# First MoE layer of a fused attention and MoE kernel: steps of group 0 in two halves around group 1, and GpSimd's part of the weight split moved to VectorE

## The chip, the cores and the metric

The kernel runs on one core of one Trainium2 chip. The metric is the device time of one execution in microseconds (us): 1056.31 us, the median of 3 runs (1056.09 to 1056.58). Engines are named as in the profile: PE is TensorE (PEld its weight loads), DVE is VectorE, ACT is ScalarE, POOL is GpSimd, SP is SyncE, which issues the DMAs spoken of here.

## The reference, cut to what matters

Three layers follow each other over 2304 tokens (4 batches of 576) of width 512: attention with a window of 64, a dense MoE layer of 2048 hidden columns with a squared relu, and a second MoE layer of 8 experts with the two best per token.

```
attn_out = _attn_ref(**attn_kwargs)                    # q, k, v: 4 x 8 heads x 576 x 64, float32
x = attn_out.transpose(0, 2, 1, 3).reshape(B * S, H * D)   # 2304 x 512
h = np.maximum(x @ w_in, 0.0)                          # first MoE: w_in 512 x 2048
x = (h * h @ w_out).astype(np.float32)                 #            w_out 2048 x 512
return _moe2_ref(x=x, **moe2_kwargs)                   # gate, noise, top 2 of 8 experts, w1, w2
```

w_in and w_out are float32 draws times a NumPy scalar of type float64, so they arrive in float64: 8 bytes a number.

## The kernel before, in words

Every matrix product is made of three products of rounded parts: an operand x is split into a rounded high part and the rest (x minus the high part), and high x high, high x rest and rest x high are added in PSUM.

**First MoE.** The tokens are cut into 6 groups of 384 (g = 0 to 5), the hidden columns into 16 blocks of 128 (f = 0 to 15). A step (g, f) has two halves. `L1(g, f)` multiplies block f of w_in with the group's tokens (12 matmuls of 384 columns into a PSUM tile "h"), then takes the relu on ACT into r, the square on ACT into the high part h[:, 0], the square again in full precision into r, and the rest h[:, 1] on DVE. `L2(g, f)` multiplies h with block f of w_out and adds to three PSUM tiles "o" (9 matmuls of 512 columns). PE's order is L1(g, f), filler, L2 of the step before, filler. After f = 15 the three sums of a group are copied to SBUF tiles "x2" and written to a DRAM tensor `x2d`, from which the second MoE gathers its rows.

**Weights.** All 32 blocks (16 of w_in, 16 of w_out; the text calls each a half) are loaded once, by `moe1_load` on SP's queue, 512 KB each, and stay in SBUF. A half is converted from float64 to float32 in `f64_to_f32` by one ACT operation (L159) and three DVE operations on integers (L160, L161, L162) into a tile "x2" or "cv", and then split by `split`: ACT writes the high part (L148), POOL the rest (L149). `weights(n)` converts halves until n are there; it is called in group 0 at the head of L1(0, f) with n = 2f + 6, so two halves are converted per step up to f = 13.

**Filler.** Between the halves of a step stand pieces of other work, taken in turn from generators: `att_group(g + 1)`, the attention of the next group (8 units of 4 pieces, each with PE, ACT, DVE and one POOL multiplication, L268), and `gating(g - 1)` of the group before. `filler(-(-left[0] // slots))` spreads what is left over the remaining slots of the group.

**What sets the order.** The Python code gives a program order; the framework then orders each engine's instructions by its own schedule. Each engine runs its queue in order and waits on semaphores.

**Second MoE.** From about 530 us: one pass after another over the experts, with POOL doing the rest of the weight split and the gathers.

Of the kernel before, what the change touches and what calls it, by code (L numbers as in the profile page):

```python
# [8 lines left out]
F32 = mybir.dt.float32  # L9
F32R = mybir.dt.float32r  # L10
# [6 lines left out]
REST = 4  # L17
# [14 lines left out]
AHEAD = 6  # L32
# [8 lines left out]
def moe_kernel(ctx, tc, q, k, v, w_in, w_out, wg, wn, noise, w1, w2, out):  # L41
    nc = tc.nc
    B, H, S, D = q.shape
    N, DM = out.shape
    E, _, F2 = w1.shape
    F = w_out.shape[0]
    NCC = DM // 128
# [96 lines left out]
                              pn[:, :N // 128 * E].rearrange("p (e t) -> p e t", e=E))  # L144


    def split(dst, src):
        nc.scalar.activation(dst[:, 0], src, AF.Copy)  # L148
        nc.gpsimd.tensor_sub(dst[:, 1], src, dst[:, 0].bitcast(F32))  # L149

    wide = w_in.dtype != F32
    if wide:
# [2 lines left out]
    def f64_to_f32(w):  # L155
        hi, lo = w[:, :, 1], w[:, :, 0]
        i = len(wres) % (3 + CVB)
        a = hw.tile([128, 512], I32, name="x2", bufs=3) if i < 3 else stg.tile([128, 512], I32, name="cv", bufs=CVB)
        nc.scalar.activation(a.bitcast(F32), hi.bitcast(F32), AF.Abs, scale=2.0 ** -112)  # L159
        nc.vector.tensor_scalar(a, a, 3, 0x7FFFFFFF, op0=OP.logical_shift_left, op1=OP.bitwise_and)  # L160
        nc.vector.scalar_tensor_tensor(a, hi, -0x80000000, a, op0=OP.bitwise_and, op1=OP.bitwise_or)  # L161
        nc.vector.scalar_tensor_tensor(a, lo, 29, a, op0=OP.logical_shift_right, op1=OP.bitwise_or)  # L162
        return a.bitcast(F32)
# [14 lines left out]
    def moe1_half(f, second):  # L178
        if 2 * f + second not in loaded:
            moe1_load(2 * f + second)  # L180
        st = loaded.pop(2 * f + second)
        w = (ringa if f < NF2 else ringb).tile([128, 2, 512], F32R, name="w")
        split(w, f64_to_f32(st.rearrange("p (a b) -> p a b", b=2)) if wide else st)
        return w

    wres = {}
# [3 lines left out]
    def weights(n):  # L190
        for x in worder[len(wres):n]:
            wres[divmod(x, 2)] = moe1_half(*divmod(x, 2))
# [100 lines left out]
    def att_group(g):  # L293
        xTs[g] = xtp.tile([128, 2, NCC, TG], F32R, name="xT")
        pool, bank = (att, ps) if g else (att0, lambda _: ps(next(late_tags if begun else start_tags)))
        lags = LAG if g else LAG0
        units = []

        def load_v(u):
            for load in late.pop(u, ()):  # L300
                load()

        for step in range(UG + max(lags)):
            for lag in lags:
                i = step - lag
                if not 0 <= i < UG:
                    continue
                if lag == 0:
                    u = g * UG + (i if g else ORD[i])
                    for x in range(u, min(u + 2, NU)) if g else ():  # L310
                        if x not in lds:
                            b, r = divmod(x, NSB * HP)
                            lds[x] = att_loads(b, r // HP, 2 * (r % HP), 2, pool)
                    if i < 2:
                        load_v(u)
                    qbd = qbds[u % 2] if g else qbds[2 + i % 4]
                    units.append(att_unit(u, lds.pop(u), xTs[g], pool, qbd, bank))
                next(units[i])
                if lag == max(lags) and g and i + 2 < UG:
                    load_v(g * UG + i + 2)  # L320
                yield
# [18 lines left out]
    def accumulate(o, steps, first, last):  # L340
        terms = [(i, t, hi, wi) for i in range(len(steps)) for hi, wis in ((0, (0, 1)), (1, (0,)))
                 for t in range(len(o)) for wi in wis]
        for i, t, hi, wi in sorted(terms, key=lambda x: (x[1], x[0])) if last else terms:
            h, w = steps[i]
            hs = h[:, hi, 128 * t:min(128 * t + 128, h.shape[2])]
            nc.tensor.matmul(o[t][:hs.shape[1]], hs, w[:, wi], start=(first and i == 0 and hi == 0 and wi == 0),  # L346
                             stop=(last and i == len(steps) - 1 and hi == 1))

    def L1(g, f):
        if g == 0:  # L350
            weights(2 * f + AHEAD)
        ph, c = begun.pop(f) if f in begun else (ps("h"), 0)
        products(ph, TG, wres[f, 0], xTs[g], range(c, NCC))
        r = hw.tile([128, TG], F32, name="r", bufs=1)
        h = hw.tile([128, 2, TG], F32R, name="h")
        nc.scalar.activation(r, ph[:, :TG], AF.Relu)  # L356
        nc.scalar.activation(h[:, 0], r, AF.Square)  # L357
        (nc.vector if g else nc.gpsimd).tensor_mul(r, r, r)  # L358
        nc.vector.tensor_sub(h[:, 1], r, h[:, 0].bitcast(F32))  # L359
        L1out[g, f] = h  # L360

    def L2(g, f):
        if f == 0:
            outs[g] = [ps("o") for _ in range(TT)]
        o = outs[g]
        accumulate(o, [(L1out.pop((g, f)), wres[f, 1])], f == 0, f == NF - 1)
        if f == NF - 1:
            x2s[g] = []
            for t in range(TT):
                x2 = hw.tile([128, DM], F32, name="x2", bufs=3)  # L370
                if t == 1:
                    nc.scalar.activation(x2, o[t], AF.Copy)
                else:
                    nc.vector.tensor_copy(x2, o[t])
                nc.sync.dma_start(x2d[TG * g + 128 * t:TG * g + 128 * t + 128, :], x2)
                x2s[g].append(x2)


# [151 lines left out]
    def stage2(e, f):  # L530
        pool = M2["stg"]
        st = pool.tile([128, 1024], F32, name="st2")
        nc.sync.dma_start(st[:, :512].rearrange("p (c f) -> p c f", c=NCC),
                          w1[e, :, 128 * f:128 * f + 128].rearrange("(c p) f -> p c f", p=128))
        nc.sync.dma_start(st[:, 512:], w2[e, 128 * f:128 * f + 128, :])
        ws = []
        for i in range(2):
            w = ringa.tile([128, 2, 512], F32R, name="w")
            split(w, st[:, 512 * i:512 * i + 512])
            ws.append(w)  # L540
        return ws

# [86 lines left out]
    def add_fill(gen, n):  # L629
        fill.append(gen)  # L630
        left[0] += n

    def filler(n):
        while n > 0 and fill:
            gen = fill.pop(0)
            try:
                next(gen)
                n -= 1
                left[0] -= 1
                fill.append(gen)  # L640
            except StopIteration:
                pass

    def drain():
        filler(10 ** 6)
        left[0] = 0

    def clear_out():
        zero = hw.tile([128, DM], F32, name="x2", bufs=3)
        nc.vector.memset(zero, 0.0)  # L650
        rows = lambda x: x.rearrange("(t p) d -> p t d", p=128)
        nc.sync.dma_start(rows(out), zero[:, None, :].to_broadcast([128, N // 128, DM]))
        nc.sync.dma_start(rows(x2d[N - TG:, :]), zero[:, None, :].to_broadcast([128, TT, DM]))
# [25 lines left out]
    att0.release()  # L679
    ringb = tc.alloc_tile_pool(name="ringb", bufs=2 * (NF - NF2), reuse_waits="tile")  # L680
    prev = None
    for g in range(NG):
        drain()
        if g == 1:
            stg.release()
            GAT["pool"] = tc.alloc_tile_pool(name="gat", bufs=1)
        if g == NG - 1:
            att.release()
            gxp = tc.alloc_tile_pool(name="gxp", bufs=1, side="right")
            gx = []  # L690
            for j in range(CT):
                t = gxp.tile([128, DM], F32, name=f"gx{j}")
                nc.vector.memset(t, 0.0)
                gx.append(t)
            M2["stg"] = tc.alloc_tile_pool(name="stg2", bufs=2, side="right")
        if g + 1 < NG:
            add_fill(att_group(g + 1), 4 * UG)
        for f in range(NF):
            if g == NG - 1 and f >= 2 and f - 2 < NF2:
                w2s[0, f - 2] = stage2(0, f - 2)  # L700
            if g == 0 and f == NF - 3:
                late_consts()
            if g == 1 and f == 8:
                clear_out()
            slots = 2 * (NF - f)
            L1(g, f)
            filler(-(-left[0] // slots))
            if prev:
                L2(*prev)
            if f == 0 and g > 0:  # L710
                add_fill(gating(g - 1), 6 + 2 * REST)
            if f == NF - 1 and g == NG - 1:
                drain()
                index_tables(0, TT)
                xA = xtp.tile([128, 2, NCC, TG], F32R, name="xT")
                add_fill(prep(list(range(TT)), xA), TT)
            filler(-(-left[0] // (slots - 1)))
            prev = (g, f)
    drain()
    L2(*prev)  # L720

# [167 lines left out]
```

## Time and profile before

| what | value |
|---|---|
| median of 3 runs | 1056.31 us |
| the profiled execution's own time | 1056.97 us |
| its span in the trace | 1055.0 us |
| PE busy over the span | 1017.3 us, 96% |
| DVE, ACT, POOL busy | 509.1, 417.8, 409.6 us |
| mean granted TensorE clock | 0.991 of full speed |

The trace covers 1055.0 us of the 1056.97 us; the other 2 us lie around it. Busy time of PE counts overlapping pipelined matmuls as one stretch. A share over the whole span is a mean over stages with different limits, so the table does not say where time can be had; stretches do.

### The profile page before, as it was taken

How to read it: one execution, taken by the hardware profiler on the slowest of the kernel's cores; microseconds unless marked ns; L12 is line 12 of the kernel's file. 1: busy time of each engine (PE TensorE's matmuls, PEld its weight loads, DVE VectorE, ACT ScalarE, POOL GpSimd, SP SyncE). 2: the span in 40 equal slices, each digit the busy share in tenths (PEclk: the TensorE clock that was granted, in tenths of full speed). 3: DMA queues.
4: the chain of work that ended last, by engine and by line, in shares of the span. 5: the costliest groups of instructions: out<-in, count | busy, mean ns of one | idle time of the engine just before them, and what ended most of it. 6: DMA issues, size and time to landing. Idle time of an engine off the chain costs nothing.

```text
span 1055.0 us, 16793 instructions
## 1 busy us (share of the span) xinstructions
PE 1017.3 (96%) x6120; PEld 899.5 (85%) x6120; DVE 509.1 (48%) x1195; ACT 417.8 (40%) x1037; POOL 409.6 (39%) x405
## 2 busy tenths in 40 slices
PE   8877799999999999999989999999999999999997
PEld 6656688889888988888878889998898998998996
DVE  7999977436645744753773642131312222231312
ACT  4664555335434443533532335332333233333210
POOL 3565631100200210110260059766565756565411
PEclk9998999999999999999999999999999999999999
DMA  9655546212112111211330326444343444443111
GB/s 200 178 160 159 164 105 235 47 30 70 39 33 78 31 39 48 54 32 23 111 111 1 110 92 194 154 140 150 117 156 106 153 134 132 128 134 121 46 47 47
DMA packets 148736, 108.33 MB, mean 103 GB/s; under 512 B 85753, under 2 KB 126713, under 8 KB 148651
## 3 DMA queue, kind: packets, MB, share of 16 engines
q1 hardware_dynamic: 139451, 80.09, 26.8%
q0 software_dynamic: 9200, 27.14, 8.2%
q8 instruction: 50, 0.82, 0.3%
q14 instruction: 35, 0.29, 0.1%
HBM read 89.27 MB, written 20.48 MB: 104 GB/s over the span
## 4 chain that ended last, share of the span: by engine, by line
PE 78%; DVE 10%; issue 6%; ACT 2%; POOL 1%; DMA 1%; POOLq 0%; SPq 0%; ACTq 0%; DVEq 0%
PE h L329 34%; PE o L346 27%; PE att L346 6%; PE att L255 2%; PE att L283 2%; DVE x L161 2%; PE att L564 2%; DVE x L162 1%; PE att L272 1%; DVE h L359 1%; DVE x L160 1%; PE att L396 1%; ACT P L265 1%; DVE r L358 1%; POOL out_dram L552 1%
## 5 line engine op out<-in xcount | busy, mean ns | idle before, releaser
L346 PE MATMUL o<-w,h 128*128 128x512 f32 x1488 | 391.4, 401 | 16.8 <-DVE h L359 12.4
L346 PEld LDWEIGHTS o<-w,h 128*128 128x128 f32 x1488 | 269.8, 189 | 74.4 <-DVE h L359 16.2
L329 PE MATMUL h<-xT,w 128*128 128x384 f32 (+1 forms) x1344 | 262.8, 343 | 3.2 <-DVE xT L287 1.9
L329 PEld LDWEIGHTS h<-xT,w 128*128 128x128 f32 x1344 | 230.4, 191 | 8.6 <-POOL w L149 2.5
L149 POOL TENSOR_TENSOR w<-st,w 128x512 fp32r<-128x512 f32 x128 | 165.1, 1301 | 104.6 <-ACT w L148 66.5
L329 PE MATMUL h<-x2T,w 128*128 128x312 f32 x1344 | 201.4, 306 | 0.0
L329 PEld LDWEIGHTS h<-x2T,w 128*128 128x128 f32 x1344 | 195.8, 188 | 3.6
L583 DVE SCALAR_TENSOR_TENSOR h<-h 128x312 fp32r<-128x312 f32 (+2 forms) x128 | 61.9, 483 | 272.7 <-ACT h L582 272.7
L148 ACT ACTIVATE w<-st 128x512 fp32r<-128x512 f32 x128 | 80.8, 631 | 191.3 <-PE att L346 119.7
L268 POOL TENSOR_TENSOR P<-P,stat 128x384 f32<-128x384 f32 x48 | 41.7, 871 | 219.4 <-DVE stat L267 103.9
L356 ACT ACTIVATE r<-h 128x384 f32<-128x384 f32 x96 | 46.7, 486 | 142.6 <-PE h L329 123.3
L582 ACT ACTIVATE h<-h 128x312 fp32r<-128x312 f32 (+2 forms) x128 | 54.4, 425 | 116.5 <-PE h L329 116.5
L346 PE MATMUL att<-w,h 128*128 128x512 f32 (+1 forms) x336 | 94.3, 393 | 0.0
L358 DVE TENSOR_TENSOR r<-r 128x384 f32<-128x384 f32 x80 | 53.0, 662 | 69.9 <-ACT h L357 68.6
L346 PEld LDWEIGHTS att<-w,h 128*128 128x128 f32 (+1 forms) x336 | 61.0, 181 | 15.4
L359 DVE TENSOR_TENSOR h<-r,h 128x384 fp32r<-128x384 f32 x96 | 60.5, 630 | 4.9 <-POOL r L358 2.2
L546 POOL DMA_INDIRECT gx<-x2d,ix x40 | 40.9, 1022 | 49.2 <-PE att L564 40.8
L552 POOL DMA_INDIRECT out_dram<-y,ix x35 | 34.4, 984 | 44.1 <-DVE y L594 37.2
L357 ACT ACTIVATE h<-r 128x384 fp32r<-128x384 f32 x96 | 50.2, 523 | 1.5
L265 ACT ACTIVATE P<-P,stat 128x128 f32<-128x128 f32 x96 | 37.6, 392 | 28.1 <-DVE stat L263 23.6
L149 POOL TENSOR_TENSOR w<-x,w 128x512 fp32r<-128x512 f32 x24 | 35.4, 1479 | 27.0 <-ACT w L148 26.8
L546 POOL DMA_INDIRECT gy<-out_dram,ix x35 | 35.6, 1016 | 19.8 <-issue 19.7
(208 smaller groups left out, 988.1 us busy)
## 6 DMA issues: line engine op xcount, KB each, us to landing
st<-in_moe_w_dram SPq DMA_DIRECT2D x128, 256.0 KB, 3.1
st<-in_moe_w_in_dram SPq DMA_DIRECT2D x16, 512.0 KB, 4.3
st<-in_moe_w_out_dram SPq DMA_DIRECT2D x16, 512.0 KB, 3.6
vn<-in_v_dram SPq DMA_DIRECT2D x110, 64.0 KB, 2.2
x2d<-x SPq DMA_DIRECT2D x18, 256.0 KB, 2.7
out_dram<-x SPq DMA_DIRECT2D x1, 4608.0 KB, 15.3
qn<-in_q_dram SPq DMA_DIRECT2D x40, 96.0 KB, 2.5
kn<-in_k_dram SPq DMA_DIRECT2D x28, 128.0 KB, 2.8
```

Source lines behind the costliest of these rows:

```text
L148: nc.scalar.activation(dst[:, 0], src, AF.Copy)
L149: nc.gpsimd.tensor_sub(dst[:, 1], src, dst[:, 0].bitcast(F32))
L265: nc.scalar.activation(P[:, j], src[:, j], AF.Exp, bias=st[:, j, 0:1], accum_out=st[:, j, 1:2])
L329: nc.tensor.matmul(p[:, :n], w[:, wi, 128 * c:128 * c + 128], x[:, xi, c], start=(c == 0 and i == 0), stop=(c == NCC - 1 and i == 2))
L346: nc.tensor.matmul(o[t][:hs.shape[1]], hs, w[:, wi], start=(first and i == 0 and hi == 0 and wi == 0), stop=(last and i == len(steps) - 1 ...
L356: nc.scalar.activation(r, ph[:, :TG], AF.Relu)
L357: nc.scalar.activation(h[:, 0], r, AF.Square)
L358: (nc.vector if g else nc.gpsimd).tensor_mul(r, r, r)
L359: nc.vector.tensor_sub(h[:, 1], r, h[:, 0].bitcast(F32))
L546: nc.gpsimd.indirect_dma_start(out=dst, out_offset=None, in_=src[:, :], in_offset=bass.IndirectOffsetOnAxis(ap=slot[i][0][:dst.shape[0]], ...
L582: nc.scalar.activation(h[:, 0, a:a + m], ph[:, :m], AF.Relu)
L583: nc.vector.scalar_tensor_tensor(h[:, 1, a:a + m], ph[:, :m], 0.0, h[:, 0, a:a + m].bitcast(F32), op0=OP.max, op1=OP.subtract)
```

## The change

Two things are changed together. First, who computes: the rest of the weight split in the first MoE (L149) goes from POOL to DVE (the second MoE's split stays on POOL), and the full-precision square becomes one DVE operation in all groups, r = h x r with h read from PSUM (it was r x r from SBUF, on POOL in group 0 and on DVE elsewhere). Second, the order: the steps run (0, 0..7), (1, 0..15), (0, 8..15), then groups 2 to 5 as before. Group 0's sums over f = 0..7 are written to `x2d`, read back at (0, 12), and added to those over f = 8..15. `weights` is called behind h, with two halves per step in (0, 0..7) and one per step from (1, 0) on. The attention of group 1 is spread over the 8 steps (0, 0..7), that of group 2 over the 8 steps (0, 8..15); group 1 has neither attention nor gating as filler. gating(1) starts at (0, 8), gating(0) at (2, 0).

```diff
-    def split(dst, src):
+    def split(dst, src, engine):
         nc.scalar.activation(dst[:, 0], src, AF.Copy)
-        nc.gpsimd.tensor_sub(dst[:, 1], src, dst[:, 0].bitcast(F32))
+        engine.tensor_sub(dst[:, 1], src, dst[:, 0].bitcast(F32))
...
     def L1(g, f):
-        if g == 0:
-            weights(2 * f + AHEAD)
...
-        (nc.vector if g else nc.gpsimd).tensor_mul(r, r, r)
+        nc.vector.tensor_mul(r, ph[:, :TG], r)
         nc.vector.tensor_sub(h[:, 1], r, h[:, 0].bitcast(F32))
         L1out[g, f] = h
+        weights(wneed.get((g, f), 0))
+
+    NH = NF // 2
+    steps = ([(0, f) for f in range(NH)] + [(1, f) for f in range(NF)] + [(0, f) for f in range(NH, NF)]
+             + [(g, f) for g in range(2, NG) for f in range(NF)])
+    wneed = {x: 2 * x[1] + AHEAD for x in steps[:NH]}
+    wneed.update({(1, f): 2 * NH + AHEAD + f for f in range(NF)})
...
+    def fetch_part():
+        for t in range(TT):
+            x2 = hw.tile([128, DM], F32, name="x2", bufs=3)
+            nc.sync.dma_start(x2, rows(0, t))
+            part.append(x2)
...
     def L2(g, f):
+        first = f == 0 or (g, f) == (0, NH)
+        last = f == NF - 1 or (g, f) == (0, NH - 1)
...
+                x2 = part[t] if part and g == 0 else hw.tile([128, DM], F32, name="x2", bufs=3)
+                if part and g == 0:
+                    nc.vector.tensor_add(x2, o[t], x2)
...
+            nxt = {(0, 0): 1, (0, NH): 2}.get((g, f), g + 1 if g > 1 else NG)
+            if nxt < NG:
+                add_fill(att_group(nxt), 4 * UG)
...
+        slots = 2 * n_left
+        L1(g, f)
+        filler(-(-left[0] // slots))
+        if prev:
+            L2(*prev)
+        if (g, f) == (0, NH + 4):
+            fetch_part()
+        done = {(0, NH): 1, (2, 0): 0}.get((g, f), g - 1 if f == 0 and g > 2 else None)
+        if done is not None:
+            add_fill(gating(done), 6 + 2 * REST)
```

The constants of the second MoE's gate (`late_consts`) move from (0, 13) to (1, 13), and the clearing of the output from (1, 8) to (2, 8). Line numbers of the changed kernel differ: L160 to L162, L148, L149, L243, L263 to L268 and L287 are the same; the square is L356 on DVE, the rest of h is L357 (L358 and L359 before).

In DVE's queue, these are the rows behind one rest of h (L359) in group 0 before the change; x and cv are the float32 tiles of a half, w its split, att and stat tiles of the attention.

```order
L359 TENSOR_TENSOR h<-r,h 128x384
L161 SCALAR_TENSOR_TENSOR cv<-st,cv 128x512
L266 TENSOR_SCALAR stat<-stat 128x3
L243 TENSOR_SCALAR qbd_106<-att 64x3x64
L162 SCALAR_TENSOR_TENSOR cv<-st,cv 128x512
L267 RECIPROCAL stat<-stat 128x3
L243 TENSOR_SCALAR qbd_106<-att 64x3x64
L160 TENSOR_SCALAR x_710<-x_710 128x512
L161 SCALAR_TENSOR_TENSOR x_710<-st,x_710 128x512
L263 TENSOR_REDUCE stat<-att 128x3
```

And this is the same queue in a step of (0, 0..7) after the change, from the rest of h (L357) to the next square (L356).

```order
L357 TENSOR_TENSOR h<-r,h 128x384
L161 SCALAR_TENSOR_TENSOR x_873<-st,x_873 128x512
L160 TENSOR_SCALAR cv<-cv 128x512
L162 SCALAR_TENSOR_TENSOR x_873<-st,x_873 128x512
L161 SCALAR_TENSOR_TENSOR cv<-st,cv 128x512
L243 TENSOR_SCALAR qbd_106<-att 64x3x64
L149 TENSOR_TENSOR w<-x_873,w 128x512
L162 SCALAR_TENSOR_TENSOR cv<-st,cv 128x512
L243 TENSOR_SCALAR qbd_106<-att 64x3x64
L263 TENSOR_REDUCE stat<-att 128x3
L149 TENSOR_TENSOR w<-cv,w 128x512
L287 TENSOR_TENSOR xT<-att,xT 128x192
```

The rest of the split (L149) now stands in DVE's queue, two instructions behind the L162 on which ACT's high part waits, and a whole attention unit stands in each step.

In PE's queue, the end of group 0 and the head of group 1 look like this before the change (L234 to L283 are attention, L387 is gating).

```order
L346 MATMUL o<-w,h 128x512 x9
L283 MATMUL att<-PT,vn 64x64 x6
L329 MATMUL h<-xT,w 128x384 x12
L234 MATMUL att<-ident,qn 128x96 x2
L236 MATMUL att<-ident,kn 128x128 x2
L346 MATMUL o<-w,h 128x512 x9
L253 LDWEIGHTS ident_b
L253 MATMUL att<-mask_89,ident_b 128x384
L255 MATMUL att<-kT,qbd_104 128x128 x3
L329 MATMUL h<-xT,w 128x384 x12
```

After the change, the head of the second half of group 0 reads as follows (L407 and L416 are gating of group 1).

```order
L346 MATMUL o<-w,h 128x512 x9
L255 MATMUL att<-kT,qbd_104 128x128 x3
L329 MATMUL h<-xT,w 128x384
L407 MATMUL att<-ident,x_1980 128x128 x4
L234 MATMUL att<-ident,qn 128x96 x2
L236 MATMUL att<-ident,kn 128x128 x2
L329 MATMUL h<-xT,w 128x384 x11
L407 MATMUL att<-ident,x_1983 128x128 x4
L255 MATMUL att<-kT,qbd_106 128x128 x3
L407 MATMUL att<-ident,x_1986 128x128 x4
```

Three pieces of filler stand there between the halves of a step where one or two stood; in group 1 between, L329 and L346 follow each other with none.

## Rows read from the trace of the kernel before

**Rows 1.** The page, part 2: busy tenths in 40 slices of 26.4 us.
```profile
PE 8877799999999999999989999999999999999997
DVE  7999977436645744753773642131312222231312
POOL 3565631100200210110260059766565756565411
```

**Rows 2.** Stretches: length, busy us of PE, PEld, DVE, ACT, POOL; clock, DMA share, GB/s.
```profile
40.00:94.60 54.60, 42.90 (x237) 34.49 (x236) 51.82 (x77) 31.69 (x84) 32.65 (x30) 0.97 0.59 172
94.60:149.00 54.40, 46.69 (x276) 38.64 (x276) 48.46 (x70) 29.52 (x74) 32.99 (x32) 0.94 0.48 132
149.00:238.00 89.00, 89.00 (x571) 78.82 (x569) 50.43 (x148) 39.37 (x114) 10.39 (x16) 1.00 0.37 110
238.00:326.80 88.80, 88.80 (x569) 78.74 (x568) 49.46 (x145) 38.86 (x113) 10.34 (x15) 1.00 0.19 47
```

**Rows 3.** Who waited for whom, 40 to 149 us: total us, times, longest.
```profile
POOL w L149 <- ACT w L148: 27.9, 15, 2.8
...
PE o L346 <- DVE h L359: 12.2, 6, 4.3
...
DVE stat L266 <- ACT P L265: 2.7, 3, 1.1
```

**Rows 4.** Groups by line and shape, 40 to 95 us: busy us, mean ns | idle before.
```profile
L149 POOL TENSOR_TENSOR w<-x,w 128x512 fp32r<-128x512 f32 x11 | 16.8, 1526 | 11.7 <-ACT w L148 11.5
L161 DVE SCALAR_TENSOR_TENSOR x<-st,x 128x512 int32<-128x512 int32 x12 | 15.1, 1258 | 0.2
...
L148 ACT ACTIVATE w<-x 128x512 fp32r<-128x512 f32 x11 | 6.9, 629 | 14.2 <-DVE x L162 14.2
...
L268 POOL TENSOR_TENSOR P<-P,stat 128x384 f32<-128x384 f32 x5 | 4.2, 833 | 5.7 <-DVE stat L267 2.9 <-ACT x L159 2.8
...
L243 DVE TENSOR_SCALAR qbd<-att 64x192 f32<-64x192 f32 x11 | 3.9, 352 | 0.2
...
L263 DVE TENSOR_REDUCE stat<-att 128x3 f32<-128x384 f32 x5 | 2.8, 561 | 0.2
```

**Rows 5.** Timeline of DVE, then of POOL, 31 to 36 us: start, us, instruction.
```profile
31.55 0.42 DVE L160 TENSOR_SCALAR x<-x 128x512 int32<-128x512 int32 x1
31.88 0.35 DVE L287 TENSOR_TENSOR xT<-att,xT 128x192 fp32r<-128x192 f32 x1
32.15 0.68 DVE L161 SCALAR_TENSOR_TENSOR x<-st,x 128x512 int32<-128x512 int32 x1
32.75 1.50 DVE L160 TENSOR_SCALAR cv<-cv 128x512 int32<-128x512 int32 x1
...
32.37 1.59 POOL L149 TENSOR_TENSOR w<-x,w 128x512 fp32r<-128x512 f32 x1 [2.16 <-ACT w L148]
```

**Rows 6.** Groups by line and shape, 590 to 800 us, then 240 to 330 us.
```profile
L583 DVE SCALAR_TENSOR_TENSOR h<-h 128x384 fp32r<-128x384 f32 x7 | 3.9, 555 | 6.1 <-ACT h L582 6.1
...
L358 DVE TENSOR_TENSOR r<-r 128x384 f32<-128x384 f32 x16 | 9.5, 596 | 11.0 <-ACT h L357 10.7
...
L391 DVE TENSOR_TENSOR x2T<-att,x2T 128x512 fp32r<-128x512 f32 x3 | 2.1, 689 | 0.2
```

**Rows 7.** Timeline of PE: L2(0,0), L2(0,7), L1(1,0), L1(2,0), a bare step's start and the next.
```profile
40.05 1.68 PE L346 MATMUL o<-w,h 128*128 128x512 f32 x6
...
94.56 0.72 PE L346 MATMUL o<-w,h 128*128 128x512 f32 x2 [0.50 <-ACT h L357]
...
149.06 0.44 PE L329 MATMUL h<-xT,w 128*128 128x384 f32 x1
...
238.01 0.51 PE L329 MATMUL h<-xT,w 128*128 128x384 f32 x2
...
560.53 2.27 PE L329 MATMUL h<-xT,w 128*128 128x384 f32 x12
...
564.72 2.27 PE L329 MATMUL h<-xT,w 128*128 128x384 f32 x12
```

More of the change, by code (lines that the diff above doesn't have):

```diff
@@ L182, in moe1_half @@
         w = (ringa if f < NF2 else ringb).tile([128, 2, 512], F32R, name="w")
-        split(w, f64_to_f32(st.rearrange("p (a b) -> p a b", b=2)) if wide else st)
+        split(w, f64_to_f32(st.rearrange("p (a b) -> p a b", b=2)) if wide else st, nc.vector)
         return w
@@ L357, in L1, with rows @@
         nc.scalar.activation(h[:, 0], r, AF.Square)
-        (nc.vector if g else nc.gpsimd).tensor_mul(r, r, r)
+        nc.vector.tensor_mul(r, ph[:, :TG], r)
         nc.vector.tensor_sub(h[:, 1], r, h[:, 0].bitcast(F32))
         L1out[g, f] = h
+        weights(wneed.get((g, f), 0))
[4 more added lines that the diff above has]
+    wneed.update({(1, f): 2 * NH + AHEAD + f for f in range(NF)})
+    part = []
+    def rows(g, t):
+        return x2d[TG * g + 128 * t:TG * g + 128 * t + 128, :]
+    def fetch_part():
[3 more added lines that the diff above has]
+            part.append(x2)
     def L2(g, f):
-        if f == 0:
+        first = f == 0 or (g, f) == (0, NH)
+        last = f == NF - 1 or (g, f) == (0, NH - 1)
+        if first:
             outs[g] = [ps("o") for _ in range(TT)]
         o = outs[g]
-        accumulate(o, [(L1out.pop((g, f)), wres[f, 1])], f == 0, f == NF - 1)
-        if f == NF - 1:
+        accumulate(o, [(L1out.pop((g, f)), wres[f, 1])], first, last)
+        if last:
             x2s[g] = []
             for t in range(TT):
-                x2 = hw.tile([128, DM], F32, name="x2", bufs=3)
-                if t == 1:
+                x2 = part[t] if part and g == 0 else hw.tile([128, DM], F32, name="x2", bufs=3)
+                if part and g == 0:
+                    nc.vector.tensor_add(x2, o[t], x2)
+                elif t == 1:
                     nc.scalar.activation(x2, o[t], AF.Copy)
@@ L374, in L2 @@
                     nc.vector.tensor_copy(x2, o[t])
-                nc.sync.dma_start(x2d[TG * g + 128 * t:TG * g + 128 * t + 128, :], x2)
+                nc.sync.dma_start(rows(g, t), x2)
                 x2s[g].append(x2)
@@ L538, in stage2 @@
             w = ringa.tile([128, 2, 512], F32R, name="w")
-            split(w, st[:, 512 * i:512 * i + 512])
+            split(w, st[:, 512 * i:512 * i + 512], nc.gpsimd)
             ws.append(w)
@@ L681, in moe_kernel @@
     prev = None
[L682 to L718, printed above, removed]
@@ new lines, in moe_kernel @@
+    left_f = {}
+    for i, (g, f) in enumerate(steps):
+        n_left = 1
+        while i + n_left < len(steps) and steps[i + n_left][0] == g:
+            n_left += 1
+        if f == 0 or (g, f) == (0, NH):
+            drain()
+            if (g, f) == (0, NH):
+                stg.release()
+                GAT["pool"] = tc.alloc_tile_pool(name="gat", bufs=1)
+            if g == NG - 1:
+                att.release()
+                gxp = tc.alloc_tile_pool(name="gxp", bufs=1, side="right")
+                gx = []
+                for j in range(CT):
+                    t = gxp.tile([128, DM], F32, name=f"gx{j}")
+                    nc.vector.memset(t, 0.0)
+                    gx.append(t)
+                M2["stg"] = tc.alloc_tile_pool(name="stg2", bufs=2, side="right")
+            nxt = {(0, 0): 1, (0, NH): 2}.get((g, f), g + 1 if g > 1 else NG)
+            if nxt < NG:
+                add_fill(att_group(nxt), 4 * UG)
+        if g == NG - 1 and f >= 2 and f - 2 < NF2:
+            w2s[0, f - 2] = stage2(0, f - 2)
+        if (g, f) == (1, NF - 3):
+            late_consts()
+        if (g, f) == (2, 8):
+            clear_out()
+        slots = 2 * n_left
[8 more added lines that the diff above has]
+            add_fill(gating(done), 6 + 2 * REST)
+        if f == NF - 1 and g == NG - 1:
+            drain()
+            index_tables(0, TT)
+            xA = xtp.tile([128, 2, NCC, TG], F32R, name="xT")
+            add_fill(prep(list(range(TT)), xA), TT)
+        filler(-(-left[0] // (slots - 1)))
+        prev = (g, f)
```

## The prediction

> **What bounds the kernel now.** The slices of the page come first: from about 130 us on PE is at 9 tenths in nearly every slice, but between 50 and 130 us it stands at 7 while DVE stands at 9 [rows 1]. So I cut the first MoE into stretches. Groups 1 and 2 take 89.0 and 88.8 us with PE busy throughout and DVE at 50 us. Group 0 does not: from L2(0,0) at 40.05 to L2(0,7) at 94.56 us DVE is busy 51.8 of 54.6 us and PE 42.9, and from there to L1(1,0) at 149.06 PE is busy 46.7 of 54.4 [rows 2, 7]. The waits tell the same: PE waited 12.2 us for DVE's last step of h [rows 3]. A bare step of PE, without filler, takes 564.72 - 560.53 = 4.19 us [rows 7], so 16 of them are 67.0 us and attention plus gating take the other 21.8 us of a full group. From L2(0,0) to L1(1,0) lie 109.0 us with 14.5 steps and one attention, 60.8 + at most 21.8 = 82.6 us of PE's work. The 26 us between are what can be had there.
>
> Why is DVE full there? Not by its own work alone. The timeline shows an integer operation of 512 columns taking 0.68 us, and the next one starting 0.60 us after it; L160 takes 0.42 us (0.33 to the next start) and L287 0.35 us (0.27). But the L160 at 32.75 us, issued while POOL runs an L149 from 32.37 to 33.96, takes 1.50 us [rows 5]. Between 40 and 95 us L161 takes 1.26 us in the mean [rows 4]. DVE operations between SBUF tiles stand still while POOL works; those that read PSUM do not (L243, from PSUM, keeps 0.35 us, L263 0.56 [rows 4]).
>
> How much? The order before gives DVE between the ends of h(0,0) and h(0,7) 14 L160, 14 L161, 14 L162, 7 L359, 11 L243, 5 each of L263, L266 and L267, and one L287. I count each by its start-to-start time, the duration less 0.08 us as in rows 5: 14 x 0.33 + 28 x 0.60 + 7 x 0.475 + 11 x 0.27 + 5 x 0.48 + 5 x 0.25 (L266 with L267, an estimate below L287's) + 0.27 = 31.6 us. Busy were 51.8, so 20.2 us were standing still against 32.65 us of POOL's work [rows 2]: 0.62 us lost on DVE per us of POOL.
>
> **The change part by part.**
>
> *Start, to L2(0,0).* Four L149 come to DVE (4 x 0.61 = 2.4 us) and four L149 with the first square leave POOL (about 6.5 us x 0.62 = 4 us). I take 0, bounds -2 to +2.
>
> *Steps (0, 0..7), DVE.* The order after has, between the same two ends of h, 12 L160, 13 L161, 13 L162, 14 L149, 7 squares from PSUM, 7 rests, 16 L243, 8 each of L263, L266 and L267, and 5 L287. L149 on DVE is not in the trace. Its nearest rows are L161 undisturbed, 0.68, and L391, also a subtraction of 512 columns, 0.689 [rows 5, 6]; I take 0.61 between starts, bounds 0.60 and 0.69. The square from PSUM times SBUF has its row in L583 at 384 columns: 0.555 us, against L358's 0.596 [rows 6], so 0.475 between starts. Sum: 4.0 + 15.6 + 8.5 + 6.65 + 4.3 + 3.8 + 2.0 + 1.35 = 46.2 us. POOL keeps 8 multiplications of 0.833 us [rows 4] and eight small memsets, about 8.7 us, which cost 8.7 x 0.62 = 5.4 us. DVE sat idle 2.8 us before; with POOL's share of the chain now its own I take 4. Total 55.6 us against 54.5: **+1.1 us**, though these 7 steps now hold all of group 1's attention where before they held some five of eight units. Below, PE bounds it: 7 x 4.19 + 21.8 = 51 us, or some 48 if the gating in the 21.8 is worth 3. Above: durations in place of starts (117 operations x 0.08 = 9), POOL's time lost whole (3), 10 us idle, together 74 us. I stay near the low side, since the value is calibrated on the same stretch. ACT (31.7 us before, three more units) and the DMA engines (0.59 of 54.6 us; about 17 us of DMA time for a whole group's attention by group 2's 0.19) stay below 45 us [rows 2].
>
> [...]
>
> *From L2(0,7) to L1(2,0).* Before: 238.01 - 94.56 = 143.45 us [rows 7]. After, PE has there what it had in group 1 (attention, one gating, 16 steps: 88.95 us) and 7.5 steps more, bare: 88.95 + 31.4 = 120.4 us. On this lies what DVE cannot keep up with. In the first 8 steps of group 1 DVE has 13 L160, 12 each of L161, L162 and L149, 16 operations of h, 2 copies of group 0's sums and 3 L287, by the same prices 35.7 us, with 2 us idle 37.7, against 33.5 of bare PE: +4.2. In the other 8 DVE has hardly a conversion left: 0. In (0, 8..15) there are three pieces of filler per slot, and the chain of gating has half the steps to hide in; DVE's work there (49.5 us of a full group less 16 operations of h, about 40) fits in 57. I take +3 for PE waits, bounds 0 and +10. Total 127.6: **-15.9 us**.
>
> *The rest at nothing.* Two more copies of sums, three adds for three copies, 0.75 MB written and read back: the copies are counted above, the transfers have over 16 steps between write and read, and the reads 4 steps before use; SP issues them among attention loads that are wanted a step later. If the x2 tiles came free late, conversions in group 1 would wait about 3 us, inside the bounds. From L1(2,0) on the work is the same, shifted; POOL against DVE at the start of the second MoE may fall otherwise by 2 us either way.
>
> *Sum.* 1.1 - 15.9 = -14.8 us on an execution of 1056.97 us (span 1055.0): 1042.2, span 1040.2. The median lies 0.66 us below that execution, so 1041.5 us.
>
> **The rivals.**
>
> *A: the wait moves into DVE, and it is slower.* POOL waited 27.9 us, 15 times, for ACT's high part before an L149: 1.86 us each [rows 3]. L149 now stands in DVE's queue, in order. If DVE waited so long in each of the 28 L149 behind h(0,0), it would lose 52 us, 4 or so hidden in group 1: about 1090 us. It decides from 14.8 / 28 = 0.53 us each; at 0.8 us, the time is 1042 + 22 = 1064. Against it: the order puts one to three operations, 0.8 us or more, between L162 and its L149, and ACT's operation takes 0.63 us [rows 4]. For it: ACT's queue is in order too, and an L148 may stand behind exponentials.
>
> *B: the first half of group 1 and the doubled filler eat it.* With (0, 0..7) at 62 us and +5 us more in the rest the time is 1042 + 6.4 + 5 = 1053 us. For it speak the upper bounds; the point at which nothing is left is a step of 10 us in (0, 0..7).
>
> *C: PE bounds all.* If DVE's standing still vanishes with POOL's work and idle stays at 2 us, (0, 0..7) takes 49 us and the later excess halves to 3.6: 1042 - 6.6 - 3.6 = 1031 us. For it: PE and DVE counts are near each other, 48 and 46.
>
> **How the numbers follow.** Forecast 0.62 (1036 to 1048), A 0.10, B 0.14, C 0.14. The range 1030 to 1055 takes in C and B and leaves out most of A and what lies beyond C, under 2 in 10. Within 0.2% (1054.2 to 1058.4) is about what a measurement of this kernel can't tell from no change; it gets B's upper end, 0.06. Slower has A, 0.10; faster the rest, 0.84.
>
> **What would show it.** In the changed trace L161 and L162 should fall to about 0.75 us in the mean, L149 on DVE stand at 0.69 and the square at 0.55 us. L2(0,7) should stand at 95 to 97 us, L1(2,0) at 222 to 225, and PE should be busy above 95% in group 1. DVE waiting over 0.5 us for each L148 means A; PE busy under 90% in (0, 8..15) means B. The sum is wrong if the 0.62 does not carry over to a stretch in which POOL is hardly busy.

## The result and the profile after

The changed kernel takes 1043.26 us, the median of 4 runs (1042.56 to 1044.06), against 1056.20 for the kernel before beside it: a ratio of 0.9878 with a 95% interval of 0.9861 to 0.9895. It is faster by 1.2%, 12.9 us; forecast were 1041.5 us and 14.8 us of gain. The profiled execution has a span of 1041.1 us.

PE's timeline of the changed kernel gives the same marks as [rows 7]: L2(0,0), L2(0,7), the fourth L1 of group 1, L1(0,8) and L1(2,0).

```profile
39.21 0.50 PE L346 MATMUL o<-w,h 128*128 128x512 f32 x1
...
89.21 0.73 PE L346 MATMUL o<-w,h 128*128 128x512 f32 x2 [1.33 <-ACT w L148]
...
109.89 2.27 PE L329 MATMUL h<-xT,w 128*128 128x384 f32 x12
...
165.48 0.33 PE L329 MATMUL h<-xT,w 128*128 128x384 f32 x1
...
223.89 0.44 PE L329 MATMUL h<-xT,w 128*128 128x384 f32 x1
```

Against before: the start gives 0.84 us (40.05 to 39.21), the steps (0, 0..7) give 4.5 us (54.5 to 50.0), the stretch from L2(0,7) to L1(2,0) gives 8.8 us (143.45 to 134.7), and from there to the end it is 817.2 us against 817.0. The sum is 13.9 us, the difference of the spans.

The stretches between these marks, with the columns of [rows 2]:

```profile
39.20:89.20 50.00, 45.97 (x297) 36.83 (x296) 49.12 (x107) 36.44 (x103) 8.16 (x14) 1.00 0.70 198
89.20:109.90 20.70, 17.91 (x102) 14.63 (x103) 18.36 (x37) 11.61 (x28) 1.24 (x2) 0.92 0.70 216
109.90:165.50 55.60, 55.60 (x283) 50.18 (x282) 34.80 (x67) 23.55 (x45) 0.33 (x1) 1.00 0.20 59
165.50:223.90 58.40, 55.65 (x394) 48.48 (x392) 38.02 (x129) 31.40 (x96) 9.57 (x14) 1.00 0.32 80
```

In (0, 0..7) DVE is as full as before, 49.1 of 50.0 us, but POOL is busy only 8.2 us where it was 32.65, and PE now 46.0 of 50.0. The second stretch, from L2(0,7) to the fourth L1 of group 1, is called the hand-over from here on: PE is busy 17.9 of 20.7 us there, and its clock falls to 0.92 in the mean. The rest of group 1 is bare steps of PE without a gap, busy 55.6 of 55.6 us.

DVE's groups by shape in (0, 0..7), which answer to [rows 4] and [rows 6]:

```profile
L162 DVE SCALAR_TENSOR_TENSOR x<-st,x 128x512 int32<-128x512 int32 x10 | 8.7, 870 | 0.0
L161 DVE SCALAR_TENSOR_TENSOR x<-st,x 128x512 int32<-128x512 int32 x10 | 8.1, 807 | 0.0
L149 DVE TENSOR_TENSOR w<-x,w 128x512 fp32r<-128x512 f32 x10 | 6.8, 680 | 0.3 <-ACT w L148 0.3
...
L356 DVE TENSOR_TENSOR r<-h,r 128x384 f32<-128x384 f32 x7 | 3.9, 550 | 0.2 <-ACT h L355 0.2
...
L160 DVE TENSOR_SCALAR x<-x 128x512 int32<-128x512 int32 x9 | 3.7, 411 | 0.0
```

On the tiles named x, L161 fell from 1.26 to 0.81 us and L160 from 0.59 to 0.41; the L149 that came to DVE takes 0.68 us where POOL's took 1.53, and waits 0.3 us in all for ACT. The square from PSUM takes 0.55 us.

About the hand-over, PE's longest waits are one for ACT's high part of a weight half, which ends as L2(0,7) starts, and three for DVE's work, 2.3 us together (waits of PE, 86 to 112 us: total, times, longest):

```profile
PE o L346 <- ACT w L148: 1.3, 1, 1.3
PE h L329 <- DVE r L356: 1.2, 1, 1.2
PE h L329 <- DVE xT L287: 1.1, 2, 0.7
```

PE's timeline shows what was left to do when L2(0,7) began, and where PE waited for xT, the attention's result:

```profile
86.83 0.44 PE L329 MATMUL h<-xT,w 128*128 128x384 f32 x1
...
89.88 0.73 PE L283 MATMUL att<-PT,vn 128*64 128x64 f32 x12
...
93.50 0.55 PE L272 MATMUL att<-ident,P 128*128 128x128 f32 x3 [0.53 <-POOL P L268]
93.98 0.73 PE L283 MATMUL att<-PT,vn 128*64 128x64 f32 x12
...
95.07 0.73 PE L283 MATMUL att<-PT,vn 128*64 128x64 f32 x12
...
96.79 2.18 PE L329 MATMUL h<-xT,w 128*128 128x384 f32 x11 [0.33 <-DVE xT L287]
99.70 1.15 PE L329 MATMUL h<-xT,w 128*128 128x384 f32 x5 [0.73 <-DVE xT L287]
102.05 3.91 PE L329 MATMUL h<-xT,w 128*128 128x384 f32 x12 [1.19 <-DVE r L356]
```

DVE's timeline shows what stands in its queue there. After the rest of h(0,7) (L357) the conversions of two halves, six operations, come ahead of the next two xT (L287); the two L149 of these halves come ahead of the last xT. ACT's part of that last xT starts at 95.84 and takes 0.33 us, but DVE's part starts only at 99.30: the L149 before it in the queue waited for ACT's high part, and that for a weight load which ended at 96.79.

```profile
92.23 0.53 DVE L357 TENSOR_TENSOR h<-r,h 128x384 fp32r<-128x384 f32 x1
92.67 1.06 DVE L160 TENSOR_SCALAR x<-x 128x512 int32<-128x512 int32 x1
93.65 0.41 DVE L160 TENSOR_SCALAR cv<-cv 128x512 int32<-128x512 int32 x1
93.99 0.68 DVE L161 SCALAR_TENSOR_TENSOR x<-st,x 128x512 int32<-128x512 int32 x1
94.59 0.68 DVE L161 SCALAR_TENSOR_TENSOR cv<-st,cv 128x512 int32<-128x512 int32 x1
95.19 0.68 DVE L162 SCALAR_TENSOR_TENSOR x<-st,x 128x512 int32<-128x512 int32 x1
95.79 0.68 DVE L162 SCALAR_TENSOR_TENSOR cv<-st,cv 128x512 int32<-128x512 int32 x1
96.40 0.61 DVE L287 TENSOR_TENSOR xT<-att,xT 128x192 fp32r<-128x192 f32 x2
98.09 0.69 DVE L149 TENSOR_TENSOR w<-x,w 128x512 fp32r<-128x512 f32 x1 [1.09 <-ACT w L148]
98.70 0.68 DVE L149 TENSOR_TENSOR w<-cv,w 128x512 fp32r<-128x512 f32 x1
99.30 0.35 DVE L287 TENSOR_TENSOR xT<-att,xT 128x192 fp32r<-128x192 f32 x1
```

In (0, 8..15) PE waits twice for the chain of gating, now under half the steps (waits of PE, 165 to 224 us):

```profile
PE att L521 <- POOL x2T L516: 1.3, 1, 1.3
PE att L477 <- DVE cm L469: 1.3, 1, 1.3
```

### The profile page after: what moved, and what is told of

It is laid out like the page before. It is cut to its first block, busy times and chain, and to the rows that moved or that the text cites. A ratio compares the mean times of both kernels' runs of the same rounds, so it can differ in the third digit from the quotient of the medians.

```text
span 1041.1 us, 16809 instructions
## 1 busy us (share of the span) xinstructions
PE 1014.9 (97%) x6120; PEld 898.5 (86%) x6120; DVE 489.1 (47%) x1246; ACT 420.5 (40%) x1037; POOL 345.2 (33%) x357
## 4 chain that ended last, share of the span: by engine, by line
PE 81%; DVE 7%; issue 5%; DMA 2%; POOL 1%; ACT 1%; SPq 0%; POOLq 0%; ACTq 0%
PE h L329 35%; PE o L346 29%; PE att L346 6%; PE att L283 2%; PE att L255 2%; PE att L584 2%; PE att L272 1%; DMA st<-in_moe_w_in_dram 1%; PE att L416 1%; PE att L407 1%; DVE w L149 1%; DVE x L162 1%; POOL out_dram L572 1%; DVE qbd L243 1%; PE att L236 1%
## 5 line engine op out<-in xcount | busy, mean ns | idle before, releaser
L346 PE MATMUL o<-w,h 128*128 128x512 f32 x1488 | 390.1, 399 | 1.3 <-ACT w L148 1.3
L346 PEld LDWEIGHTS o<-w,h 128*128 128x128 f32 x1488 | 270.1, 188 | 54.5 <-ACT w L148 1.6
L329 PE MATMUL h<-xT,w 128*128 128x384 f32 (+1 forms) x1344 | 262.6, 341 | 2.3 <-DVE r L356 1.2
L329 PEld LDWEIGHTS h<-xT,w 128*128 128x128 f32 x1344 | 231.0, 190 | 9.2 <-DVE xT L287 1.8
L329 PE MATMUL h<-x2T,w 128*128 128x312 f32 x1344 | 201.4, 306 | 0.0
L149 POOL TENSOR_TENSOR w<-st,w 128x512 fp32r<-128x512 f32 x128 | 164.7, 1297 | 104.3 <-ACT w L148 66.6
L329 PEld LDWEIGHTS h<-x2T,w 128*128 128x128 f32 x1344 | 195.8, 188 | 3.6
L148 ACT ACTIVATE w<-st 128x512 fp32r<-128x512 f32 x128 | 80.8, 631 | 190.3 <-PE att L346 120.0
L268 POOL TENSOR_TENSOR P<-P,stat 128x384 f32<-128x384 f32 x48 | 40.9, 853 | 233.2 <-DVE stat L267 126.9
L346 PE MATMUL att<-w,h 128*128 128x512 f32 (+1 forms) x336 | 94.3, 393 | 0.0
L356 DVE TENSOR_TENSOR r<-h,r 128x384 f32<-128x384 f32 x96 | 53.2, 554 | 81.8 <-ACT h L355 80.3
L346 PEld LDWEIGHTS att<-w,h 128*128 128x128 f32 (+1 forms) x336 | 61.0, 181 | 15.4
L357 DVE TENSOR_TENSOR h<-r,h 128x384 fp32r<-128x384 f32 x96 | 56.8, 591 | 3.0
L243 DVE TENSOR_SCALAR qbd<-att 64x192 f32<-64x192 f32 x86 | 30.3, 352 | 24.3 <-PE att L236 23.4
```

The costliest lines, as they stand in the source:

```text
L149: engine.tensor_sub(dst[:, 1], src, dst[:, 0].bitcast(F32))
L329: nc.tensor.matmul(p[:, :n], w[:, wi, 128 * c:128 * c + 128], x[:, xi, c], start=(c == 0 and i == 0), stop=(c == NCC - 1 and i == 2))
L356: nc.vector.tensor_mul(r, ph[:, :TG], r)
```

## Experiments

The theory behind the prediction is called R: what group 0 loses is DVE standing still while POOL works, and the gain comes from taking POOL's work away. Its rival, O: the order of steps is what counts, since it halves the rate of conversions. The median of before was 1056.20 us beside the full change and 1057.26 to 1057.51 us in these runs, on four chips, so kernels are compared by their ratios to the kernel before.

| run | order of steps | what is on DVE | us | ratio to before, interval |
|---|---|---|---|---|
| e2_order_only | new | nothing more | 1060.94 | 1.0037, 1.0024 to 1.0049 |
| e11_behind_h_only | old, conversions behind h | nothing more | 1055.84 | 0.9977, 0.9966 to 0.9988 |
| e7b_square_only | old, conversions behind h | square | 1049.60 | 0.9919, 0.9903 to 0.9936 |
| e7a_split_only | old, conversions behind h | rest of split | 1039.70 | 0.9834, 0.9818 to 0.9851 |
| e1_engines_only | old | both | 1043.63 | 0.9864, 0.9848 to 0.9881 |
| e1b_engines_behind_h | old, conversions behind h | both | 1040.28 | 0.9838, 0.9817 to 0.9858 |
| the full change | new | both | 1043.26 | 0.9878, 0.9861 to 0.9895 |
| e5_square_from_sbuf | new | both, square from SBUF | 1045.48 | 0.9896, 0.9871 to 0.9920 |
| e4_attention_earlier | new | both | 1044.52 | 0.9869, 0.9844 to 0.9895 |
| e3_later_halves | new, later halves | both | 1038.45 | 0.9816, 0.9793 to 0.9839 |
| e34_both | new, later halves, attention earlier | both | 1037.11 | 0.9813, 0.9790 to 0.9835 |
| e6_weights_on_pool_queue | new | both, loads on POOL's queue | 1056.69 | 0.9995, 0.9983 to 1.0007 |

**The engines alone, and the order alone.** e1 makes these edits to the kernel before and leaves the order:

```diff
-        nc.gpsimd.tensor_sub(dst[:, 1], src, dst[:, 0].bitcast(F32))
+        engine.tensor_sub(dst[:, 1], src, dst[:, 0].bitcast(F32))
...
-        (nc.vector if g else nc.gpsimd).tensor_mul(r, r, r)
+        nc.vector.tensor_mul(r, ph[:, :TG], r)
```

with VectorE handed to `split` in the first MoE and GpSimd in the second. Expected:

> The order of steps of before, with the two moves to VectorE alone (rest of the weight split in the first MoE, full-precision square from PSUM); weights are still converted ahead of each step of group 0. Theory R (GpSimd standing in VectorE's way is the cost): from L2(0,0) to L1(1,0) VectorE has 26 L160, 53 of L161 and L162, 26 L149, 30 operations of h and 8 attention units, 8.6 + 31.8 + 15.9 + 14.3 + 12.3 = 83 us, with 3.7 us lost to GpSimd and 2 us idle 89 us against 109 before: 1036 to 1042 us, at least as fast as the full change. Rival O (the order is what counts, since two halves per step up to step 13 keep VectorE the bound): 1047 to 1053 us.

e1b moves the conversions behind h as well:

```diff
-        if g == 0:
-            weights(2 * f + AHEAD)
...
         L1out[g, f] = h
+        if g == 0:
+            weights(2 * f + AHEAD)
```

> As e1_engines_only, and the conversions stand behind h in the program, as in the full change. Both theories: the framework orders the queues itself, so within 2 us of e1_engines_only. If the place in the program matters by itself (h comes earlier in VectorE's queue), 3 us or more below it.

e2 is the full change with the engines of before:

```diff
-        split(w, f64_to_f32(st.rearrange("p (a b) -> p a b", b=2)) if wide else st, nc.vector)
+        split(w, f64_to_f32(st.rearrange("p (a b) -> p a b", b=2)) if wide else st, nc.gpsimd)
...
-        nc.vector.tensor_mul(r, ph[:, :TG], r)
+        (nc.vector if g else nc.gpsimd).tensor_mul(r, r, r)
```

> The new order of steps with the engines of before (GpSimd has the rest of the split, and the square of group 0). Theory R: (0, 0..7) has 34 us of VectorE's own work and 33 us of GpSimd's, of which 0.62 is lost, 58 us against 50 in the full change, and the hand-over to group 1 loses 3 us more: 1051 to 1058 us, nearly nothing gained over before. Rival O: 1043 to 1048 us.

The engines alone give the whole gain, 0.9864 where the full change has 0.9878; the order alone makes the kernel slower, 1.0037. Rival O falls. Both runs came out worse than R had put them: e2 2.9 us above R's range and e1 1.6 us above. In its profiled run e2 takes from about L2(0,0) to L2(0,7) 63.6 us where R put 58, with POOL busy 35.7 and DVE 51.7:

```profile
39.00:102.60 63.60, 50.72 (x329) 42.48 (x329) 51.73 (x92) 37.00 (x110) 35.74 (x37) 0.95 0.55 155
```

Here DVE is not even full: besides the standing still it has 11.9 us of idle time, of which it waits 6.7 us for POOL's square.

e1b stands 2.6 parts in a thousand below e1, but the intervals overlap; in the profiled runs L1(2,0) stands 3.4 us earlier (222.0 against 225.4). From L2(0,0) to L1(1,0) before took 109.0 us, e1 takes 98.0 and e1b 93.5 (e1, then e1b):

```profile
38.40:136.40 98.00, 86.36 (x511) 69.46 (x510) 89.46 (x190) 61.97 (x156) 11.49 (x17) 1.00 0.60 170
...
38.90:132.40 93.50, 85.84 (x510) 68.35 (x508) 90.35 (x186) 62.90 (x154) 12.37 (x17) 1.00 0.62 179
```

R had put 89 us for e1, with 2 us of idle time on DVE; it is idle 8.5 us. Where POOL's work is gone, the same operations of DVE are shorter. These are L161 and L162 on the tiles x, before and then e1b, in this stretch:

```profile
L161 DVE SCALAR_TENSOR_TENSOR x<-st,x 128x512 int32<-128x512 int32 x20 | 21.8, 1098 | 0.3
L162 DVE SCALAR_TENSOR_TENSOR x<-st,x 128x512 int32<-128x512 int32 x21 | 20.4, 979 | 0.2
...
L161 DVE SCALAR_TENSOR_TENSOR x<-st,x 128x512 int32<-128x512 int32 x20 | 14.2, 715 | 0.0
L162 DVE SCALAR_TENSOR_TENSOR x<-st,x 128x512 int32<-128x512 int32 x21 | 14.2, 678 | 0.0
```

**Which of the two moves, and the place of the conversions.** All three on the old order with conversions behind h: e7a keeps the square of group 0 on POOL, e7b keeps the rest of the split there, e11 both. The edit of e7a against e1b, and that of e7b:

```diff
-        nc.vector.tensor_mul(r, ph[:, :TG], r)
+        (nc.vector if g else nc.gpsimd).tensor_mul(r, r, r)
```

```diff
-        split(w, f64_to_f32(st.rearrange("p (a b) -> p a b", b=2)) if wide else st, nc.vector)
+        split(w, f64_to_f32(st.rearrange("p (a b) -> p a b", b=2)) if wide else st, nc.gpsimd)
```

> As e1b_engines_behind_h (old order, 1040 us), but only the rest of the weight split is moved to VectorE; the square of group 0 stays on GpSimd. Theory R by its price: 15 squares of about 1 us of GpSimd between L2(0,0) and L1(1,0), 0.4 to 0.62 of it lost on VectorE, 6 to 10 us, against 7 us of VectorE's own that go: 1039 to 1044 us. If what counts is the longer way of h over GpSimd (ACT, GpSimd, VectorE, then L2), every step gets later: 1046 us or more.

> As e1b_engines_behind_h, but only the square is moved; the rest of the split stays on GpSimd. Theory R by its price: 26 splits of 1.3 to 1.5 us of GpSimd between L2(0,0) and L1(1,0), 0.62 of it lost on VectorE, 21 to 24 us, against 16 us of VectorE's own that go: 1045 to 1050 us. If the split alone carries the gain: 1052 us or more.

> The kernel before with one edit: the weights are converted behind h instead of ahead of it; order of steps and engines as before. Theory R: GpSimd's 65 us of work in group 0 stay and go on standing in VectorE's way, so 1053 to 1058 us (1057.5 for before on this chip), and the 8 us of e7b_square_only come mostly from the square. If the place in the program is worth as much as it was on top of the engines (3 us of 1043.6) or more, 1050 to 1054 us.

Their stretches from L2(0,0) to L1(1,0), e7a, e7b and e11 in this order:

```profile
38.10:131.50 93.40, 85.94 (x511) 69.33 (x510) 87.34 (x173) 62.60 (x156) 32.55 (x33) 1.00 0.61 177
```

```profile
40.20:143.90 103.70, 89.34 (x513) 72.75 (x512) 98.73 (x162) 60.67 (x156) 53.39 (x45) 0.95 0.56 160
```

```profile
40.40:147.60 107.20, 91.76 (x513) 75.28 (x512) 93.94 (x145) 60.86 (x156) 69.56 (x61) 0.92 0.54 155
```

All three fell within what R gave. The split alone carries the gain: e7a takes 93.4 us in this stretch, e1b 93.5. With the split on DVE, the square on POOL adds 20.2 us of POOL's work (32.55 against 12.37) and takes a net 13 operations from DVE, 6.5 us by the prediction's prices; DVE's busy time falls by 3.0 us, so 3.5 us are lost, 0.2 per us of POOL and not 0.62. The same reckoning for the square with the split on POOL (e11 against e7b) gives 0.2 again, and for the split it gives about 0.6 both times (e7b against e1b, e11 against e7a).

With the split on POOL, moving the square is worth 6.2 us (1055.84 to 1049.60); with the split on DVE it is worth nothing that these runs can tell (0.9838 against 0.9834). So the two moves do not add up: where the one has made DVE free, the other buys nothing. The conversions behind h alone give 0.9977, a small gain with an interval clear of 1.

**The square's operand.**

```diff
-        nc.vector.tensor_mul(r, ph[:, :TG], r)
+        nc.vector.tensor_mul(r, r, r)
```

> The full change, with the square as r x r from SBUF instead of h x r with h in PSUM. Theory R: with GpSimd quiet in groups 0 and 1 the square takes 0.56 us either way, so within 1.5 us of the full change (1042 to 1045). [...] If the PSUM operand is what keeps the square out of GpSimd's way, L356 rises above 0.65 us in (0, 0..7) and the time is 1046 or more.

0.9896 against 0.9878: the median, 1045.48 us, lies 0.5 us above what R gave, but the intervals overlap, so this run can tell no difference. The square itself takes 0.552 us from SBUF in (0, 0..7), where the full change has 0.550 from PSUM:

```profile
L356 DVE TENSOR_TENSOR r<-r 128x384 f32<-128x384 f32 x7 | 3.9, 552 | 0.2 <-ACT h L355 0.2
```

So the PSUM operand is not what kept the square short here.

**The hand-over.** There are two theories for the 20.7 us from L2(0,7) to the fourth L1: D, conversions ahead in DVE's queue, with their loads; T, the serial tail of group 1's attention. e3 takes conversions away there:

```diff
-    wneed = {x: 2 * x[1] + AHEAD for x in steps[:NH]}
-    wneed.update({(1, f): 2 * NH + AHEAD + f for f in range(NF)})
+    wneed = {x: min(2 * x[1] + AHEAD, 2 * NH + 1) for x in steps[:NH]}
+    wneed.update({(1, f): 2 * NH + 2 + f for f in range(1, NF)})
```

> The full change with fewer weight conversions about the hand-over from group 0 to group 1: none in (0, 6), (0, 7) and (1, 0) beyond the 17 halves that group 0 needs there, then one per step of group 1. In the full change the hand-over (L2(0,7) to the fourth L1 of group 1, 20.7 us for 12.6 us of bare steps and some 4 us of attention) loses about 4 us. Theory D (conversions ahead in VectorE's queue, and their loads, make the hand-over late): the 4 us and 2 to 4 us of (0, 6) and (0, 7) go, 1036 to 1040 us. Theory T (the serial tail of group 1's attention, exponentials to xT, makes it late): within 1.5 us of the full change.

e4 ends the attention two steps earlier:

```diff
-        slots = 2 * n_left
+        slots = max(1, 2 * n_left - 4) if g == 0 and f < NH else 2 * n_left
...
-        filler(-(-left[0] // (slots - 1)))
+        filler(-(-left[0] // max(1, slots - 1)))
```

> The full change with group 1's attention spread over the slots of 6 steps instead of 8, so that its tail lies beside (0, 6) and (0, 7). Theory T: the hand-over's 4 us go, 1038 to 1041 us. Theory D: VectorE is as full as before and the steps (0, 0..5) get longer by what the hand-over gains, within 1.5 us of the full change.

e34 makes both edits:

> e3 and e4 together. Theory D and T both right: 1034 to 1038 us, below the old order with the engines moved (1040). Theory D alone: as e3. If neither counts, 1042 to 1045 us, and the new order has no advantage over the old one with the same engines.

e3 is faster, 0.9816, its interval apart from the full change's. e4 is not, and e34 adds nothing to e3 that the intervals can tell. D holds, T falls. In e3 the hand-over takes 15.3 us, 5.4 less, and the steps around it are as they were, so the 2 to 4 us that D had put in (0, 6) and (0, 7) did not come:

```profile
39.10:89.20 50.10, 46.47 (x311) 37.96 (x310) 48.14 (x107) 35.54 (x105) 9.62 (x15) 1.00 0.69 196
89.20:104.50 15.30, 14.65 (x87) 12.27 (x88) 12.85 (x27) 9.96 (x22) 1.12 (x1) 1.00 0.74 215
104.50:160.10 55.60, 55.60 (x282) 50.18 (x282) 39.81 (x77) 25.49 (x49) 1.89 (x1) 1.00 0.27 81
```

The clock is at 1.00 where it was 0.92. Of the 5.4 us, 1.1 are work of PE that now lies before L2(0,7). Whether the conversions' operations on DVE, their ACT parts or their loads count most was not separated.

In e4 the tail did move: all of group 1's last products lie before L2(0,7), and the hand-over takes 14.6 us. But (0, 0..7) takes 56.3 us, 6.3 more, so what the one gains the other loses, as D said:

```profile
39.30:95.60 56.30, 51.59 (x347) 42.26 (x346) 50.60 (x114) 39.13 (x113) 11.06 (x16) 0.97 0.65 185
95.60:110.20 14.60, 10.65 (x44) 8.79 (x44) 14.32 (x27) 8.16 (x15) 0.00 (x0) 0.89 0.64 221
```

The conversions that e3 takes out lie now beside the bare steps, where DVE's 39.8 us (34.8 in the full change) cost nothing: this is what the new order is good for, and the full change did not use it. With it the new order stands at 0.9816 and 0.9813 against 0.9834 and 0.9838 for the old one; the intervals overlap, so an advantage of the order is not shown. e3 and e34 have the lowest medians of this study, and the kernel before and the full change are both slower by more than the intervals.

**Loads on another queue.** The chain of what ended last shows two weight loads about the hand-over, 4.9 us from 82.28 and 3.7 us from 93.14, so e6 issues them from POOL:

```diff
-            nc.sync.dma_start(st, w_out[128 * f:128 * f + 128, :])
+            nc.gpsimd.dma_start(st, w_out[128 * f:128 * f + 128, :])
```

and the same for w_in.

> The full change with the weight loads of the first MoE issued on GpSimd's queue instead of SP's, where they stand behind attention loads that wait for buffers. If loads in SP's queue are what the hand-over waits for (the chain of what ended last has 8.6 us of these loads between 82 and 97 us), it goes: 1037 to 1041 us. If not, GpSimd's work for 32 issues costs VectorE time instead: 1043 to 1048 us.

That was a miss in size: 1056.69 us, 0.9995, 8.7 us above the range. Of the 13.3 us by which the profiled run is longer than the full change's, half lies ahead of the stretches looked at: L2(0,0) stands at 45.9 us, 6.7 later. (0, 0..7) takes 53.0 us, 3.0 more, with POOL busy 17.5 us instead of 8.2, and the bare steps of group 1 take another 3 us more:

```profile
45.90:98.90 53.00, 46.26 (x297) 36.81 (x297) 48.72 (x106) 35.40 (x101) 17.50 (x27) 1.00 0.59 168
```

The hand-over takes 20.7 us as in the full change, so taking the loads off SP's queue does not shorten it. That its wait was not for loads is not shown by this run, since on POOL's queue the loads meet waits of their own: 9.2 us for DVE's L162 between 39 and 110 us. Why the start is late was not tried; the waits there show DVE waiting 8.0 us for PE's attention scores.

## Why the prediction was right

The total was right, 1041.5 against 1043.3 us, well inside 1030 to 1055, and the mechanism held; that the total came so close is in part luck, since two errors of 5.6 and 7.1 us nearly cancel. L1(2,0) was put at 222 to 225 us and stands at 223.9; L2(0,7) was put at 95 to 97 and stands at 89.2. Point by point:

- *What bounds group 0.* Right, and shown: with the order unchanged and the conversions behind h, taking the split off POOL makes 93.4 us of 107.2 (e7a against e11), though DVE then has 28 operations more.
- *Start*, 0 with bounds of 2: measured -0.84.
- *(0, 0..7)*, forecast +1.1 (55.6 us): measured -4.5 (50.0). The mechanism was right and three sizes were off. Between the new marks lie 107 operations of DVE (12 L160, 13 each of L161, L162 and L149, 14 of h, 16 L243, 8 L263, 7 each of L266 and L267, 4 L287), 45.1 us by the prices of the prediction, against 46.2. POOL's 8.16 us cost 49.1 - 45.1 = 4.0 us, 0.49 per us, where 0.62 was carried over and 5.4 us were put; a price that is off by 0.01 us moves this 0.49 by 0.13. The largest miss is the idle time: DVE idled 0.9 us where 4 were given. So the sign of being wrong that the prediction named, the 0.62, was off by less than the allowance for idle time.
- *From L2(0,7) to L1(2,0)*, forecast -15.9 (127.6 us): measured -8.8 (134.7). PE had more to do there than counted: at L2(0,7) only one of 12 matmuls of L1(1,0) was done, which leaves 2.1 us, and three units of attention's last products (0.73 us each) and one of transposes (0.55) had not been done, 2.7 us. The forecast had these 4.8 us ahead of L2(0,7). (0, 0..7) was bound by DVE, busy 49.1 of 50.0 us, so they are not why it ended early; that its 5.6 us and the 7.1 us here have opposite signs is luck. Beyond PE's work 7.2 us were forecast and about 9.5 measured: 5.4 in the hand-over (20.7 less 12.6 of bare steps and 2.7), 1.1 at the constants of the gate, 3.1 in (0, 8..15) where 3 were put and 2.6 of PE's waits on gating are seen. Of the 5.4 us PE stood idle 2.8; the lower clock took part of the rest, since the 12 matmuls from 102.05 took 3.91 us at a granted clock of 0.56 and those from 109.89 2.27 us at 1.00. The +4.2 for DVE behind PE in group 1 was near in size, but it fell on the hand-over alone and not over 8 steps.
- *The rest at nothing.* 817.2 against 817.0 us.
- *Rival A*, the wait in DVE: DVE waited 0.3 us for L148 in (0, 0..7) and 1.3 us in the hand-over, far below 0.53 us each. But one wait of 1.09 us stands ahead of the last xT in the hand-over, where PE waits behind it. *B* did not come: the second half of group 0 has PE busy 95%. *C* was nearer for (0, 0..7), 50.0 against its 49.
- *A slip in the bounds.* The upper bound counts 117 operations; the prediction's own list has 111, which is 0.5 us less.
- *What the prediction did not ask* is which half of the change earns the sum. It costed the order and the engines as one; the runs show that the engines earn all of it, and that the order as written costs 0.4% with both moves (the full change against e1b) and 0.6% without them (e2 against e11), the intervals apart both times, until its conversions are put beside the bare steps.

## What to carry to other kernels

When an engine reads as full, compare the duration of one of its operations alone with the mean in the full stretch: here 0.68 against 1.26 us said that the cure was not less work for VectorE but less beside it on GpSimd, and giving VectorE 28 operations more made group 0 14 us shorter (e7a against e11). A change of two parts is costed part by part, and each alone is run: here one part was worth all, and the other was a loss as it was written. When work is spread over more steps, look at the seam: conversions left in the two steps around it cost about 5 us, and the same conversions beside bare PE steps nothing.

## What the runs showed of the hardware that was not expected

What GpSimd's work costs VectorE depended on which operation it was. On the old order with conversions behind h, the rest of the split (two SBUF inputs, 512 columns) on GpSimd cost VectorE about 0.6 us per us of GpSimd, and the square (384 columns) 0.2, each in two pairs of runs. This is not the whole of it: the kernel before, with the same two operations on GpSimd as e11 but its conversions ahead of h, loses 0.60 per us where e11 loses 0.48 (DVE's busy 100.2 and 93.9 us, less 60.9 us for its 144 operations at the prediction's prices), and why was not tried.

A square of 384 columns on VectorE took the same time with one operand in PSUM (0.550 us) as with both in SBUF (0.552), where the two rows in the prediction stood 0.04 us apart (0.555 for L583, 0.596 for L358).

PE's granted clock, on the old order from L2(0,0) to L1(1,0), was 0.92 to 0.95 in the three runs with the split on GpSimd and 1.00 in the three with it on VectorE; PE's busy time for the same matmuls is 89.5 us before and 85.8 in e1b. On the new order it fell with the split on VectorE too, to 0.92 in the hand-over of the full change, where PE stood idle 2.8 of 20.7 us.

Issuing 32 loads of 512 KB from GpSimd made the kernel 13 us slower than issuing them from SyncE; the loads took GpSimd's time, 17.5 us busy in (0, 0..7) against 8.2.
